# One PSUM copy moved from ScalarE to VectorE, and four row tiles given other memory, in a fused attention and expert kernel

## The chip, the cores and the metric

The kernel runs on one core of one Trainium2 chip. A core has a matrix engine (TensorE, PE in the profile), two engines for elementwise work (VectorE, DVE; ScalarE, ACT), GpSimd (POOL), and a queue engine (SyncE, SP) that here only issues transfers. Each engine works through its own list of instructions in order; semaphores make one wait for another. The metric is the device time of one execution in microseconds.

## The reference

Sliding-window attention with a linear distance bias over 8 batches, 8 heads, 576 positions and 64 channels, and behind it a top-1 mixture of 8 experts over the 4608 tokens, everything in float32:

```python
scores = q @ k.T / sqrt(64) - slope[h] * |i - j|      # only 0 <= i - j < 128
attn   = softmax(scores) @ v                           # (B, H, S, D) -> x (B*S, H*D)
logits = x @ w_gate                                    # 4608 x 8
e      = argmax(logits);  gate_w = softmax(logits)[e]
y      = gate_w * (relu(x @ w1[e]) @ w2[e])            # w1: 512 x 1024, w2: 1024 x 512
```

## The kernel before

**Units.** Attention is cut into 16 units: 4 pairs of batches (`bp`) times 4 pairs of heads (`hp`). A unit has four steps, `g` = 0 to 3. `scores` (L800) multiplies keys and queries into a PSUM tile `sp`; ScalarE takes the exponentials out of it (L811, L816) into `pe`; VectorE multiplies them by distance factors (`weigh`, L830); `values` (L857) multiplies them by V into the PSUM tile `at`. The queries of a unit are taken in two halves of 320 and 256 positions. The first half is complete in step 2, the second in step 3. There is one `at` tile, so the second half's matmuls may not begin before the first half has been copied out. `finish` does that: L874 copies 128 x 640 floats (first half) or 128 x 384 (second half) into `xT`, and L876 the remaining 128 columns of the second half. `sums` (L894) then has TensorE add up the exponentials, and VectorE collects the sums (L907).

**Order.** The order is written by hand: `tc.manual_schedule()` keeps each engine's instructions as the Python code emits them. The main loop emits, per step, the scores of steps ahead, this step's values, and one entry of a list of `tasks`. Steps 0, 1 and 3 take an entry at their end; step 2 takes one just behind `finish` of the first half. So what a step 1 takes stands ahead of that copy on every engine.

**Tasks.** When a pair is done, the tasks of the pair are spread over the following pair's 16 steps (`behind`): gate logits (`gate`, L915 on TensorE and L920, L922 on VectorE), turned by TensorE (`turn`, L939) and copied (L940), then VectorE chains: softmax scales (`scale_a`, L948 onward; `scale_a2`, L969 and L973), the choice of the expert, counting and slots, one-hot tables (`ones_at`, L1063 and L1069; `ones_at2`, L1078), and the rows of `x` written to DRAM. In the first pair the rows are made by VectorE transposes (`squares_turned`, L1158), a small GpSimd copy (L1166) and four transfers of GpSimd's queue for each row tile (`squares_out`, L1177); eight of the nine row tiles take buffers in turn out of a pool of five named `xs`, and the ninth (t = 8) does too. In the later pairs TensorE and ScalarE make the rows (L1107, L1109). `xT` has two buffers, so the third pair's first copy overwrites what the first pair's transposes read.

**The end of attention.** After three pairs the tokens of the first expert are listed (`early_table`, L1100 and L1195 to L1201) and gathered by GpSimd into a tile `s` (L1324). VectorE scales each gathered tile (`to_scale`, L1343), TensorE turns it (L1366), ScalarE copies it (L1367), VectorE forms sums of it (L540 to L543), and the first expert begins (L1619, Strassen's seven products instead of eight). One scaling is a task of the last unit's step 1. The tile `s` has one buffer, which held index numbers at the program's start and nothing from there until this gather.

**The experts.** The rest is seven blocks of matmuls for the experts (L1619, L1684) with their sums on VectorE. `general_path`, the fallback for other routings, is compiled in and not executed.

## Time and profile before

| | |
|---|---|
| median of 3 runs | 637.21 us (635.33 to 641.54) |
| profiled execution | 639.93 us, its span 638.2 us |
| TensorE busy | 603.6 us, 95% of the span |
| VectorE, ScalarE, GpSimd busy | 59%, 33%, 41% |
| granted TensorE clock | 0.993 of full speed |
| attention | 4 to 167 us of the span |

The profile has a page of totals, a list of groups of instructions with the idle time ahead of them, tables of who waited for whom, sums by stretches of time, and a timeline. A timeline row reads: start in us, duration in us (several merged instructions end together), engine, line, operation, tiles written and read, shape and count, and in brackets the time that the engine stood idle before and who ended it. The first matmuls of `values` of unit 4 start at 46.6 us, those of unit 8 at 84.0, of unit 12 at 128.1, of unit 15 at 161.7.

### The profile page before, as it was taken

What the parts mean: (1) busy time and instruction counts of PE and PEld (TensorE: products, weight loads), DVE (VectorE), ACT (ScalarE), POOL (GpSimd) and SP (SyncE); (2) the same over time, 40 slices, a digit from 0 to 9 for tenths busy, and PEclk for the clock granted to TensorE, in tenths of its full rate; (3) what the DMA queues carried; (4) which work ended last, traced back from release to release, by engine and by line L of the source; (5) the groups of instructions that cost most, each with busy time, mean ns of one, the idle gap of its engine ahead of it and who ended that gap; (6) DMA issues with size and microseconds to landing.
All of it is one profiled execution on the core that took longest, in us unless ns stands there. A gap on an engine that the chain in (4) does not pass through costs nothing.

```text
span 638.2 us, 13413 instructions
## 1 busy us (share of the span) xinstructions
PE 603.6 (95%) x5204; PEld 480.9 (75%) x5204; DVE 378.6 (59%) x731; ACT 213.8 (33%) x456; POOL 261.5 (41%) x452
## 2 busy tenths in 40 slices
PE   5889989999889999999999999999999999999995
PEld 4766767777688986777666677777777778999884
DVE  3345966678769682485548455665565575586511
ACT  5767747677332122310330032113202311311310
POOL 8200473405203304873663376258515624840022
PEclk9999999999989999999999999999999999999998
DMA  9895897996605673760466047514822470460212
GB/s 239 232 239 172 239 249 205 368 242 207 200 2 137 189 251 92 288 210 13 91 196 213 17 88 201 212 31 103 299 78 66 132 283 24 103 229 17 46 61 70
DMA packets 80332, 101.09 MB, mean 158 GB/s; under 512 B 41699, under 2 KB 57219, under 8 KB 80259
## 3 DMA queue, kind: packets, MB, share of 16 engines
q1 hardware_dynamic: 68722, 72.08, 38.9%
q0 software_dynamic: 10384, 27.18, 13.8%
q8 instruction: 43, 0.70, 0.5%
q10 hardware_dynamic: 1152, 0.88, 0.5%
q14 instruction: 31, 0.25, 0.1%
HBM read 72.54 MB, written 19.30 MB: 144 GB/s over the span
## 4 chain that ended last, share of the span: by engine, by line
PE 73%; DVE 6%; DMA 5%; issue 5%; ACT 4%; SPq 3%; POOL 2%; POOLq 0%; ACTq 0%; DVEq 0%
PE trio L1684 29%; PE trio L1619 28%; PE sp L800 4%; PE at L857 4%; SPq L1719 3%; PE m L894 3%; DMA q_sb<-in_qT_dram 3%; DMA x_rows<-xs 2%; ACT pe L816 1%; PE m L1107 1%; PE trio L1787 1%; PE trio L1799 1%; ACT pe L811 1%; POOL out_dram L1727 1%; PE m L915 1%
## 5 line engine op out<-in xcount | busy, mean ns | idle before, releaser
L1324 POOL DMA_INDIRECT xg<-x_rows,p_idx x110 | 117.6, 1069 | 29.8 <-issue 26.0
L1610 DVE TENSOR_TENSOR h<-trio,s 128x624 f32<-128x624 f32 (+6 forms) x48 | 35.9, 748 | 92.8 <-PE trio L1619 92.2
L1619 PE MATMUL trio<-xgT,w 128*128 128x312 f32 (+5 forms) x336 | 87.4, 410 | 0.7 <-ACT z L1805 0.7
L1684 PE MATMUL trio<-h,w 128*128 128x312 f32 (+5 forms) x320 | 80.6, 409 | 0.0
L1619 PEld LDWEIGHTS trio<-xgT,w 128*128 128x128 f32 x336 | 63.8, 190 | 20.3 <-ACT z L1805 1.5
L1684 PEld LDWEIGHTS trio<-h,w 128*128 128x128 f32 x320 | 62.5, 196 | 16.0
L830 DVE TENSOR_TENSOR pe<-pe,x 128x512 f32<-128x512 f32 x64 | 43.4, 686 | 33.8 <-ACT pe L811 33.5
L800 PE MATMUL sp<-q_sb,k_sb 64*64 64x192 f32 (+2 forms) x1152 | 55.3, 322 | 8.4 <-DMA q_sb<-in_qT_dram 7.3
L1611 ACT ACTIVATE h<-h 128x624 f32<-128x624 f32 (+6 forms) x48 | 32.6, 678 | 90.9 <-DVE h L1610 90.9
L857 PE MATMUL at<-pe,v_sb 64*64 64x192 f32 (+2 forms) x1408 | 54.4, 284 | 5.5 <-ACT xT L874 3.8
L1619 PE MATMUL trio<-xs,ws 128*128 128x312 f32 (+5 forms) x224 | 57.5, 410 | 0.0
L1684 PE MATMUL trio<-hs,w2s 128*128 128x312 f32 (+5 forms) x224 | 55.8, 407 | 0.0
L857 PEld LDWEIGHTS at<-pe,v_sb 64*64 64x64 f32 x1408 | 45.0, 134 | 13.2 <-ACT xT L874 6.3
L800 PEld LDWEIGHTS sp<-q_sb,k_sb 64*64 64x64 f32 x1152 | 40.0, 137 | 18.4 <-ACT pe L816 4.2
L1619 PEld LDWEIGHTS trio<-xs,ws 128*128 128x128 f32 x224 | 42.6, 190 | 12.6
L1684 PEld LDWEIGHTS trio<-hs,w2s 128*128 128x128 f32 x224 | 43.6, 196 | 10.6
L811 ACT ACTIVATE pe<-sp 128x512 f32<-128x512 f32 x64 | 38.7, 604 | 26.0 <-PE sp L800 21.2
L816 ACT ACTIVATE pe<-sp,mid 128x128 f32<-128x128 f32 x128 | 40.4, 377 | 0.0
L1727 POOL DMA_INDIRECT out_dram<-x,s_idx x19 | 20.5, 1078 | 41.6 <-DMA x<-zo 34.9
L1727 POOL DMA_INDIRECT out_dram<-zo,s_idx x19 | 21.8, 1149 | 25.9 <-DVE zo L1772 15.0
L1619 PE MATMUL trio<-xgT,ws 128*128 128x312 f32 (+5 forms) x112 | 29.9, 410 | 0.0
L1619 PE MATMUL trio<-xs,w 128*128 128x312 f32 (+5 forms) x112 | 29.9, 410 | 0.0
(257 smaller groups left out, 927.0 us busy)
## 6 DMA issues: line engine op xcount, KB each, us to landing
w<-in_moe_w_dram SPq DMA_DIRECT2D x15, 2048.0 KB
k_sb<-in_kT_dram SPq DMA_DIRECT2D x15, 576.0 KB
q_sb<-in_qT_dram SPq DMA_DIRECT2D x15, 576.0 KB
v_sb<-in_v_dram SPq DMA_DIRECT2D x14, 320.0 KB
x_rows<-xs POOLq DMA_DIRECT2D x16, 264.0 KB, 4.8
v_sb<-in_v_dram SPq DMA_DIRECT2D x14, 256.0 KB
zo<-x SPq DMA_DIRECT2D x88, 40.0 KB
w<-in_moe_w_dram SPq DMA_DIRECT2D x5, 512.0 KB
```

The costliest lines, as they stand in the source:

```text
L800: nc.tensor.matmul(by_distance(sp[c * KB : (c + 1) * KB, r, :GC], kb, 0, n), lhsT=k_sb[u][hs, c, kb * KB : (kb + 1) * KB], rhs=q_sb[u][hs, ...
L811: nc.scalar.activation(outer, sp[:, :, :GC].rearrange("p r (j x) -> p r j x", j=3)[:, :, 0:3:2, :], AF.Exp, scale=SCALE,)
L816: nc.scalar.activation(pe[:, r, 1, :], sp[:, r, inner], AF.Exp, bias=mid[:, h0 + r : h0 + r + 1], scale=SCALE,)
L830: nc.vector.tensor_tensor(outer, outer, fac[:, h0 : h0 + 2, : 2 * w].rearrange("p r (j x) -> p r j x", j=2)[:, :, :, : 2 * KB], op=ALU.mult,)
L857: nc.tensor.matmul(acc[r * D : (r + 1) * D, c, lo - q0 : hi - q0].rearrange("p (j x) -> p j x", x=KB), lhsT=v_sb[u // 2][c * KB : (c + 1) ...
L894: nc.tensor.matmul(sm[at_row : at_row + 32, to], lhsT=ind[:, hp, :], rhs=x[:, r, 2, last] if j is None else x[:, r, j, k0 * KB : k1 * KB], ...
L1324: nc.gpsimd.indirect_dma_start(out=to, out_offset=None, in_=where, in_offset=bass.IndirectOffsetOnAxis(ap=idx, axis=0),)
L1610: nc.vector.tensor_tensor(to, ps, u, op=ALU.add)
L1611: nc.scalar.activation(to, to, AF.Relu)
L1619: nc.tensor.matmul(banks[k][:, f, :n2], lhsT=left[m][:, d, fb * P : (fb + 1) * P], rhs=right[m][:, d, :], start=(m in (1, 2, 5) and d == 0 ...
L1684: nc.tensor.matmul(banks[k][:, c, :n2], lhsT=left[m][:, f, c::2], rhs=right[m][:, f, :], start=(m in (1, 2, 5) and f == 0), stop=True, ski ...
L1727: ins = nc.gpsimd.indirect_dma_start(out=out[:, :], out_offset=bass.IndirectOffsetOnAxis(ap=s_idx[:w, g["c0"] + j : g["c0"] + j + 1], axis=0),
```

## The change

The copy of a unit's first half (128 x 640 floats out of PSUM, 16 of them) is done by VectorE instead of ScalarE; the second half's copies stay on ScalarE. Of the first pair's nine row tiles, t = 4 to 7 are turned into one tile of the memory named `s`, which the first expert's gather uses later; t = 0 to 3 and t = 8 keep the pool of five. Number and order of the transfers stay as they are.

```diff
@@ finish
-            nc.scalar.copy(xT[bp][:, hp, : 2 * LQ].rearrange("p (b q) -> p b q", b=2)[:, :, q0 : q0 + n], acc[:, :, :n])
+            copy = nc.vector.tensor_copy if half == 0 else nc.scalar.copy
+            copy(xT[bp][:, hp, : 2 * LQ].rearrange("p (b q) -> p b q", b=2)[:, :, q0 : q0 + n], acc[:, :, :n])
@@ squares
-                if bp in spare and t < TPB - 1:
+                if bp == 0 and 4 <= t < TPB - 1:
+                    if t == 4:
+                        spare[bp] = mx_pool.tile([P, 4, NA, PW], F32, name="s")
+                    xs_of[bp, t] = spare[bp][:, t - 4]
+                elif bp in spare and t < TPB - 1:
```

Where the copy stands in VectorE's list is shown at three places. Lines behind L874 are higher by one in the changed kernel, behind L1149 by five. First VectorE in unit 5 (second unit of the second pair), before, from the multiplication of step 1 on:

```order
L830 TENSOR_TENSOR pe<-pe,x_138 128x2x2x128
L969 RECIPROCAL r<-s 128x72
L973 TENSOR_TENSOR pr<-gsr,r 128x9x32 x2
L982 TENSOR_TENSOR pr<-pr 128x9x32
L983 TENSOR_TENSOR pr<-pr 128x9x16
```

and now:

```order
L830 TENSOR_TENSOR pe<-pe,x_138 128x2x2x128
L970 RECIPROCAL r<-s 128x72
L974 TENSOR_TENSOR pr<-gsr,r 128x9x32 x2
L875 COPY xT<-at 128x2x320
L983 TENSOR_TENSOR pr<-pr 128x9x32
```

The copy stands behind step 1's task (the reciprocal and two products) and ahead of step 2's. Second, VectorE in unit 7 (last unit of the second pair), before, with the tables (`at_col`, `oc`, and `gsr`, the memory of the row table) and the first pair's row transposes:

```order
L1063 TENSOR_TENSOR at_col<-cols_b,rc 128x432
L1069 TENSOR_TENSOR oc<-at_col,tok 128x432 x2
L830 TENSOR_TENSOR pe<-pe,x_138 128x2x2x128
L1078 TENSOR_TENSOR gsr<-cols_b,rc 128x1152
L1158 STREAM_TRANSPOSE xs<-xT 128x4x128 x2
L830 TENSOR_TENSOR pe<-pe,x_138 128x2x2x128 x2
```

and now:

```order
L1064 TENSOR_TENSOR at_col<-cols_b,rc 128x432
L1070 TENSOR_TENSOR oc<-at_col,tok 128x432 x2
L830 TENSOR_TENSOR pe<-pe,x_138 128x2x2x128
L1079 TENSOR_TENSOR gsr<-cols_b,rc 128x1152
L875 COPY xT<-at 128x2x320
L1163 STREAM_TRANSPOSE s<-xT 128x4x128 x2
L830 TENSOR_TENSOR pe<-pe,x_138 128x2x2x128 x2
```

The copy stands behind the 1152-wide row table, and the transposes of t = 4 and 5 write `s`. Third, VectorE in the last unit, before, with the weight sums (`ws`, `w`) and the first scaling of gathered rows (`xn<-s`):

```order
L830 TENSOR_TENSOR pe<-pe,x_138 128x2x2x128 x2
L1343 TENSOR_TENSOR xn<-s 128x512
L534 TENSOR_TENSOR w_1995<-w_1995 128x512
L907 TENSOR_TENSOR sum_of_163<-m,sum_of_163 64x320
L907 TENSOR_TENSOR sum_of_163<-m,sum_of_163 64x256
```

and now:

```order
L830 TENSOR_TENSOR pe<-pe,x_138 128x2x2x128 x2
L1348 TENSOR_TENSOR xn<-s 128x512
L875 COPY xT<-at 128x2x320
L534 TENSOR_TENSOR w_1992<-w_1992 128x512
L908 TENSOR_TENSOR sum_of_163<-m,sum_of_163 64x320
L908 TENSOR_TENSOR sum_of_163<-m,sum_of_163 64x256
```

The copy stands behind the scaling, which needs the gather's landing. On TensorE, GpSimd and SyncE the order is the same in both kernels; ScalarE's list is the old one without the 16 copies.

## The prediction

> **What bounds the kernel now.** The page's totals come first, then its chain of waits by engine.

> ```profile
> PE 603.6 (95%) x5204; PEld 480.9 (75%) x5204; DVE 378.6 (59%) x731; ACT 213.8 (33%) x456; POOL 261.5 (41%) x452
> PE 73%; DVE 6%; DMA 5%; issue 5%; ACT 4%; SPq 3%; POOL 2%; POOLq 0%; ACTq 0%; DVEq 0%
> ```

> TensorE sets the time, so a change is worth what it takes from TensorE's idle time, or adds to it. Both edits lie in attention, the first 169 us. The table of waits for TensorE from 20 to 175 us says what its idle time there waits for (us in total, times, longest).

> ```profile
> PE at L857 <- ACT xT L874: 3.8, 8, 0.9
> PE m L939 <- DVE gs L920: 2.2, 2, 2.0
> PE m L1366 <- DVE xn L1343: 1.9, 1, 1.9
> ```

> The first line is the copy that changes engine: at 8 of 16 units the second half's matmuls wait for it, 3.8 us in all. The sums by stretches (PE, PEld, DVE, ACT, POOL busy) show how full the two engines are.

> ```profile
> 20.00:40.00 20.00, 17.67 (x467) 14.90 (x460) 9.92 (x18) 15.45 (x45) 0.01 (x1) 1.00 0.92 222
> 60.00:80.00 20.00, 18.13 (x454) 14.99 (x450) 18.23 (x49) 14.55 (x41) 7.62 (x16) 1.00 0.84 238
> ```

> Ahead of the first pair's tasks VectorE is half free (9.92 of 20 us). From 60 to 80 us it is the fuller engine, 18.23 of 20 us, and three units copy there.

> **What the copy costs.** Groups by shape (count, busy us, mean ns):

> ```profile
> L874 ACT COPY xT<-at 128x640 f32<-128x640 f32 x16 | 11.3, 704 | 2.7 <-DVE xs L1158 1.8 <-PE at L857 0.8
> L920 DVE TENSOR_TENSOR gs<-m,sum_of 128x512 f32<-128x512 f32 x8 | 5.5, 689 | 3.6 <-PE m L915 3.6
> L922 DVE TENSOR_TENSOR gs<-m,sum_of 128x128 f32<-128x128 f32 x4 | 1.1, 283 | 0.0
> L907 DVE TENSOR_TENSOR sum_of<-m,sum_of 64x320 f32<-64x320 f32 x12 | 5.8, 482 | 12.6 <-PE m L894 12.6
> L671 DVE CAST pe<-s 128x320 f32<-128x320 int32 x1 | 0.3, 334 | 2.4 <-POOL s L663 2.4
> ```

> ScalarE loses 16 x 0.70 = 11.3 us. VectorE has no 640-wide copy out of PSUM, so its price is bounded: from L922 to L920, both out of PSUM, 384 elements cost 406 ns, 1.06 ns each, and 128 more than L920's give 689 + 135 = 824 ns. Two of the 320-wide casts would be 0.67 us, two of L907's 0.96. I take 0.82 (L920 is nearest), so VectorE gains 13.1 us. [...]

> **Where the copy is no longer late.** With a free VectorE it starts when the first half is done. In unit 2:

> ```profile
> 31.71 0.22 PE L857 MATMUL at<-pe,v_sb 64*64 64x64 f32 x1
> 32.34 0.69 DVE L830 TENSOR_TENSOR pe<-pe,x 128x512 f32<-128x512 f32 x1 [1.03 <-ACT pe L811]
> 32.68 0.73 ACT L874 COPY xT<-at 128x640 f32<-128x640 f32 x1
> 33.46 1.55 PE L857 MATMUL at<-pe,v_sb 64*64 64x64 f32 x48 [0.88 <-ACT xT L874]
> ```

> The half is done at 31.93; ScalarE, busy with exponentials, copies from 32.68. VectorE is free then and its multiplication at 32.34 now stands behind the copy (it is for the next unit, some 4 us later, which hides the delay). Copy 31.99 to 32.81, the matmuls at 32.86 instead of 33.46: gain 0.60. Units 1 and 3 have the same form:

> ```profile
> 24.00 1.55 PE L857 MATMUL at<-pe,v_sb 64*64 64x64 f32 x48 [0.44 <-ACT xT L874]
> 39.19 0.84 PE L857 MATMUL at<-pe,v_sb 64*64 64x192 f32 x24
> 41.23 0.56 PE L857 MATMUL at<-pe,v_sb 64*64 64x64 f32 x15 [0.56 <-ACT xT L874]
> ```

> Unit 1 gains its whole 0.44; unit 3, whose half is done at 39.19 + 0.84 = 40.03 and would be copied by 40.91, gains 0.27. Together 1.3. Units 0, 4, 8 and 13 show no idle time of TensorE for the copy and keep none.

> **Where it now stands behind a task.** VectorE works in order, and step 1's task is ahead of the copy. Unit 5:

> ```profile
> 61.63 0.83 DVE L973 TENSOR_TENSOR pr<-gsr,r 128x288 f32<-128x288 f32 x2
> 61.86 1.55 PE L857 MATMUL at<-pe,v_sb 64*64 64x64 f32 x48 [0.56 <-ACT xT L874]
> ```

> The products end at 62.46; the copy, overlapping their end by 0.07 as VectorE's rows do, ends at 63.2, and the matmuls start at 63.25 instead of 61.86: loss 1.4. Unit 7:

> ```profile
> 79.79 1.35 DVE L1078 TENSOR_TENSOR gsr<-cols_b,rc 128x1152 bf16<-128x1152 bf16 x1
> 78.80 0.89 PE L857 MATMUL at<-pe,v_sb 64*64 64x64 f32 x24 [0.15 <-ACT xT L874]
> 79.92 0.89 PE L857 MATMUL at<-pe,v_sb 64*64 64x192 f32 x24 [0.24 <-DVE pe L830]
> ```

> The row table ends at 81.14, the copy at 81.9, so 78.80 becomes 81.94: 3.1 lost, 2.9 with the 0.24 wait at 79.92 that is then long over. Behind it queue the multiplications for unit 8 and L907, which VectorE catches up while TensorE stands.

> **The row tiles.** Here the second edit enters:

> ```profile
> 87.14 1.07 PE L915 MATMUL m<-xT,wgd 128*32 128x512 f32 x8
> 88.94 0.71 DVE L1158 STREAM_TRANSPOSE xs<-xT 128x512 f32<-128x512 f32 x1 [1.67 <-DMA x_rows<-xs]
> 90.14 0.68 DVE L920 TENSOR_TENSOR gs<-m,sum_of 128x512 f32<-128x512 f32 x1
> 90.88 0.66 PE L939 MATMUL m<-ident,gs 128*128 128x128 f32 x4 [2.04 <-DVE gs L920]
> ```

> The transpose of t = 8 waits 1.67 us for the transfer that empties t = 3's buffer; L920 is queued behind it and TensorE's L939 behind that, idle 2.04. Now t = 8 is only the fifth tile of its pool and waits for nothing. GpSimd still issues the same transfers in the same order, and the tile `s` is idle until its gather, at 161 us. So the second edit alone could return 2.0. Next late is the gate itself: delayed by 2.9, L915 ends at 88.21 + 2.9 = 91.1, L920 at 91.85, and L939 starts at 91.9 instead of 90.88. Of unit 7's 2.9 us, 1.0 remains.

> **The remaining units.** Unit 11 has a row table ahead again:

> ```profile
> 119.58 1.35 DVE L1078 TENSOR_TENSOR gsr<-cols_b,rc 128x1152 bf16<-128x1152 bf16 x1
> 121.33 1.25 PE L857 MATMUL at<-pe,v_sb 64*64 64x64 f32 x33
> ```

> It ends at 120.93, the copy at 121.68: 0.4 lost. For units 6, 9, 10 and 12, where task or copy ends within 0.2 us of TensorE's next matmuls, I estimate 0.3 together. Units 14 and 15:

> ```profile
> 157.45 1.55 PE L857 MATMUL at<-pe,v_sb 64*64 64x64 f32 x48 [0.16 <-ACT xT L874]
> 157.79 0.17 DVE L1201 CAST s_idx<-tb 128x4 int32<-128x4 f32 x1
> 161.16 1.06 POOL L1324 DMA_INDIRECT s<-x_rows,g_idx  x1 [3.86 <-DVE sum_of L907]
> 164.06 1.55 PE L857 MATMUL at<-pe,v_sb 64*64 64x64 f32 x48 [0.85 <-ACT xT L874]
> 165.59 0.69 DVE L1343 TENSOR_TENSOR xn<-s 128x512 f32<-128x512 f32 x1 [1.95 <-DMA s<-x_rows,g_idx]
> ```

> In unit 14 the eight small instructions of the first expert's list end at 157.96; the copy ends at 158.72 and TensorE is 1.3 late. In unit 15 the scaling L1343 waits for the gather until 165.59. It ends at 166.28, the copy at 167.03, and the last matmuls of attention start at 167.08 instead of 164.06. The gather hangs on the rows and the list, both ahead of unit 14's copy, so it does not shift with the 1.3: both units together lose 3.0. The tail keeps it:

> ```profile
> 167.11 0.94 DVE L907 TENSOR_TENSOR sum_of<-m,sum_of 64x320 f32<-64x320 f32 x2 [0.23 <-PE m L894]
> 168.69 1.29 DVE L1343 TENSOR_TENSOR xn<-s 128x512 f32<-128x512 f32 x2
> 169.53 0.63 PE L1366 MATMUL m<-ident,xn 128*128 128x128 f32 x4 [1.89 <-DVE xn L1343]
> ```

> The next scaling stands behind L907, which waits for the last sums on TensorE, 3.0 later too. The experts behind are bound by TensorE and carry it to the end.

> **Sum.** -1.3 + 1.4 + 1.0 + 0.4 + 0.3 + 3.0 = +4.8 us, 0.75%. The profiled execution took 639.93 us with a span of 638.2; it would be 644.7. It lies 2.7 above the median of the runs, which becomes 637.21 + 4.8 = 642.0.

> **Rivals.** First, faster: VectorE reaches the copies in time, so all 3.8 us of waits go, and 2.0 at the row tiles: -5.8, 631.4 us. It decides where step 1's task ends before the first half does; units 1 to 3 speak for it, the rows at 79.79 and 165.59 against. Chance 0.12. Second, no change to speak of: the 3.0 us at the end are taken back, because the first expert's start has waits of its own (1.89 at 169.53 is one): +1.8, 639.0. The order through L907 speaks against. Chance 0.18. Third, slower than forecast: unit 7's 2.9 is kept whole, because VectorE, full from 60 to 80 us, enters unit 8 as late as TensorE does (+1.9), and the copy costs 0.96 (0.14 at 7 places, +1.0): +7.7, 644.9. L907's waits of 12.6 us in all speak against, since VectorE catches up there. Chance 0.15. Nothing suggests that the edits do not do what they say; the order shows both.

> **Numbers.** The forecast has 0.55. One per cent is 6.4 us, about what a measurement tells from no change. Two of the copies at 0.67 instead of 0.82 and the runs' own spread (635.33 to 641.54) put it between 638.5 and 645.5. The range 636.0 to 646.0 holds forecast, second and third rival and leaves out the first and some of the third's tail. Slower by over 1% (643.6) takes a quarter of the forecast and most of the third rival, 0.26; faster by over 1% half of the first, 0.06; within 1% the rest, 0.68.

> **What would show it.** The 640-wide copy as a VectorE group near 0.82 us; TensorE's waits at L857 for VectorE's copy near 1.4 (unit 5), 3 (unit 7), 1.4 and 2.5 us (units 14, 15) and none in units 1 to 3; no wait of the t = 8 transpose for a transfer; attention ending 4 to 5 us later. It is wrong if these copies end within 0.2 us of where ScalarE's did, or if the first expert's sums (L540) start as early as before.

## The result and the profile after

The changed kernel took 647.65 us, the median of 5 runs (645.78 to 649.93), against 637.21 us before, which is now also the median of 5: a ratio of 1.0145, 95% interval 1.0115 to 1.0174. (Ratios here leave out disturbed runs, so they need not be the quotients of the medians.) The forecast was 642.0 us with a range from 636.0 to 646.0. The direction was right, the result lies above the range, and the loss was about twice the 0.75% forecast. The profiled execution took 647.65 us, its span is 645.9, against 639.93 and 638.2: 7.7 us more where +4.8 was forecast.

The page's totals and its chain by engine, the table of waits from 20 to 175 us, and the copy's group:

```profile
PE 607.9 (94%) x5204; PEld 482.9 (75%) x5204; DVE 389.9 (60%) x747; ACT 204.4 (32%) x440; POOL 259.7 (40%) x452
PE 76%; DVE 8%; issue 5%; SPq 3%; DMA 2%; ACT 2%; POOL 1%; POOLq 0%; ACTq 0%; DVEq 0%
...
PE at L857 <- DVE xT L875: 10.1, 8, 3.4
...
L875 DVE COPY xT<-at 128x640 f32<-128x640 f32 x16 | 13.1, 822 | 5.6 <-PE at L857 5.4
```

The copy costs what was forecast, 0.822 us. TensorE's wait for it grew from 3.8 to 10.1 us in as many places (8), the longest from 0.9 to 3.4. TensorE's busy time grew too, by 4.3 us, although it executes the same 5204 matmuls; 2.6 us of that lie in unit 7, as shown below. Matmuls that take longer are what the prediction did not have.

Where a task stands ahead of the copy, the timeline shows the row that the order foretold. Unit 2 (VectorE free), unit 5, and units 14 and 15:

```profile
31.62 0.82 DVE L875 COPY xT<-at 128x640 f32<-128x640 f32 x1 [0.64 <-PE at L857]
32.50 1.55 PE L857 MATMUL at<-pe,v_sb 64*64 64x64 f32 x48 [0.30 <-DVE xT L875]
...
60.98 0.83 DVE L974 TENSOR_TENSOR pr<-gsr,r 128x288 f32<-128x288 f32 x2
61.72 0.82 DVE L875 COPY xT<-at 128x640 f32<-128x640 f32 x1
62.59 1.22 PE L857 MATMUL at<-pe,v_sb 64*64 64x64 f32 x32 [1.94 <-DVE xT L875]
...
163.39 0.82 DVE L875 COPY xT<-at 128x640 f32<-128x640 f32 x1
164.26 1.55 PE L857 MATMUL at<-pe,v_sb 64*64 64x64 f32 x48 [1.44 <-DVE xT L875]
...
170.62 0.69 DVE L1348 TENSOR_TENSOR xn<-s 128x512 f32<-128x512 f32 x1 [0.17 <-DMA s<-x_rows,g_idx]
171.34 0.82 DVE L875 COPY xT<-at 128x640 f32<-128x640 f32 x1
172.22 1.55 PE L857 MATMUL at<-pe,v_sb 64*64 64x64 f32 x48 [2.19 <-DVE xT L875]
```

Unit 7 and the gate behind it:

```profile
80.81 1.34 DVE L1079 TENSOR_TENSOR gsr<-cols_b,rc 128x1152 bf16<-128x1152 bf16 x1
82.19 0.82 DVE L875 COPY xT<-at 128x640 f32<-128x640 f32 x1
83.07 2.84 PE L857 MATMUL at<-pe,v_sb 64*64 64x64 f32 x48 [3.44 <-DVE xT L875]
85.84 2.79 PE L895 MATMUL m<-pe,ind 128*32 128x320 f32 x28
92.91 0.70 DVE L1163 STREAM_TRANSPOSE xs<-xT 128x512 f32<-128x512 f32 x1
95.40 0.66 PE L940 MATMUL m<-ident,gs 128*128 128x128 f32 x4 [0.18 <-DVE gs L921]
96.68 1.50 PE L857 MATMUL at<-pe,v_sb 64*64 64x64 f32 x48
```

The wait of 3.44 us is the one forecast, and so is the end of the gate's wait: the transpose of t = 8 waits for nothing, and L940 for 0.18 us instead of 2.04. (Whether the row tiles did that is seen below, where the copies move alone.) But the two groups of matmuls behind the wait took 2.84 and 2.79 us. The same 48 matmuls of unit 14 took 1.55, and the 28 of the sums 1.51 there. The sums by stretches show why; the granted clock is the third number from the end of each row. Before, then after:

```profile
80.00:100.00 20.00, 17.63 (x366) 13.02 (x370) 12.64 (x27) 11.08 (x30) 16.09 (x33) 1.00 0.91 241
```

```profile
80.00:100.00 20.00, 16.75 (x305) 12.18 (x305) 13.21 (x22) 7.34 (x21) 15.66 (x34) 0.83 0.86 232
81.70:88.60 6.90, 5.53 (x77) 4.29 (x78) 3.67 (x6) 0.65 (x2) 4.46 (x11) 0.51 0.89 250
```

TensorE's clock was halved for 6.8 us, from inside the wait until 88.5 us. (2.84 - 1.55) + (2.79 - 1.51) = 2.6 us were lost on work that waits for nothing. That is more than the gate gave back: from unit 7's second half to unit 8's it took 96.68 - 83.07 = 13.61 us. Before it took 92.17 - 78.80 = 13.37:

```profile
92.17 1.50 PE L857 MATMUL at<-pe,v_sb 64*64 64x64 f32 x48
```

The lag of the changed kernel, that is, how much later than before the second halves' matmuls start in the two timelines: -1.21 us at unit 3, -0.65 at unit 4, +0.73 at unit 5, +4.27 at unit 7, +4.51 at unit 8, +5.37 at unit 11, +5.38 at unit 13, +6.81 and +8.16 at units 14 and 15, +7.8 at the first expert's sums and +7.75 at the end.

### The profile page after: what moved, and what is told of

Same layout as the page of the kernel before. It is cut to its first block, busy times and chain, and to the rows that moved or that the text cites. A ratio compares the mean times of both kernels' runs of the same rounds, so it can differ in the third digit from the quotient of the medians.

```text
span 645.9 us, 13410 instructions
## 1 busy us (share of the span) xinstructions
PE 607.9 (94%) x5204; PEld 482.9 (75%) x5204; DVE 389.9 (60%) x747; ACT 204.4 (32%) x440; POOL 259.7 (40%) x452
## 3 DMA queue, kind: packets, MB, share of 16 engines
q10 hardware_dynamic: 1152, 0.88, 0.5%
## 4 chain that ended last, share of the span: by engine, by line
PE 76%; DVE 8%; issue 5%; SPq 3%; DMA 2%; ACT 2%; POOL 1%; POOLq 0%; ACTq 0%; DVEq 0%
PE trio L1689 29%; PE trio L1624 27%; PE at L857 6%; PE sp L800 5%; PE m L895 3%; SPq L1724 3%; PE m L1108 1%; DVE xT L875 1%; PE trio L1792 1%; PE trio L1804 1%; PE m L916 1%; DMA q_sb<-in_qT_dram 1%; POOL out_dram L1732 1%; DVE pe L830 1%; DVE xT L1163 1%
## 5 line engine op out<-in xcount | busy, mean ns | idle before, releaser
L1624 PE MATMUL trio<-xgT,w 128*128 128x312 f32 (+5 forms) x336 | 87.4, 410 | 0.7 <-ACT z L1810 0.7
L1624 PEld LDWEIGHTS trio<-xgT,w 128*128 128x128 f32 x336 | 63.8, 190 | 20.3 <-ACT z L1810 1.5
L857 PE MATMUL at<-pe,v_sb 64*64 64x192 f32 (+2 forms) x1408 | 56.3, 290 | 11.9 <-DVE xT L875 10.1
L857 PEld LDWEIGHTS at<-pe,v_sb 64*64 64x64 f32 x1408 | 45.9, 138 | 21.1 <-DVE xT L875 14.3
L830 DVE TENSOR_TENSOR pe<-pe,x 128x512 f32<-128x512 f32 x64 | 43.3, 686 | 24.2 <-ACT pe L811 23.9
L1624 PE MATMUL trio<-xs,ws 128*128 128x312 f32 (+5 forms) x224 | 57.5, 410 | 0.0
L1624 PEld LDWEIGHTS trio<-xs,ws 128*128 128x128 f32 x224 | 42.6, 190 | 12.6
L811 ACT ACTIVATE pe<-sp 128x512 f32<-128x512 f32 x64 | 38.5, 601 | 31.9 <-PE sp L800 26.9
L1624 PE MATMUL trio<-xs,w 128*128 128x312 f32 (+5 forms) x112 | 29.9, 410 | 0.0
L1624 PE MATMUL trio<-xgT,ws 128*128 128x312 f32 (+5 forms) x112 | 29.9, 410 | 0.0
```

The source lines that it names most:

```text
L811: nc.scalar.activation(outer, sp[:, :, :GC].rearrange("p r (j x) -> p r j x", j=3)[:, :, 0:3:2, :], AF.Exp, scale=SCALE,)
L830: nc.vector.tensor_tensor(outer, outer, fac[:, h0 : h0 + 2, : 2 * w].rearrange("p r (j x) -> p r j x", j=2)[:, :, :, : 2 * KB], op=ALU.mult,)
L857: nc.tensor.matmul(acc[r * D : (r + 1) * D, c, lo - q0 : hi - q0].rearrange("p (j x) -> p j x", x=KB), lhsT=v_sb[u // 2][c * KB : (c + 1) ...
L1624: nc.tensor.matmul(banks[k][:, f, :n2], lhsT=left[m][:, d, fb * P : (fb + 1) * P], rhs=right[m][:, d, :], start=(m in (1, 2, 5) and d == 0 ...
```

## The experiments

The theory that the two profiles suggest: VectorE's order makes the waits as forecast, and the wait of 3.4 us in unit 7 has a second price, the halved clock behind it, which takes what the row tiles give. Rivals: the row edit returns nothing; the wait alone is the loss, whatever the clock does; the loss lies mostly elsewhere (units 14 and 15). Four groups of four kernels, each group beside the kernel before on its own chip (the first group has no run of the changed kernel):

| kernel | median, us | before, us | ratio (95% interval) |
|---|---|---|---|
| row tiles alone | 649.74 | 649.46 | 0.9989 (0.9950 to 1.0029) |
| copies alone | 655.73 | 649.46 | 1.0105 (1.0065 to 1.0146) |
| changed, unit 7's copy on ScalarE | 651.23 | 649.46 | 1.0040 (1.0023 to 1.0057) |
| changed, unit 7's wait filled | 650.03 | 649.46 | 1.0031 (1.0004 to 1.0057) |
| changed | 653.61 | 648.64 | 1.0071 (1.0030 to 1.0113) |
| changed, units 14 and 15 on ScalarE | 655.92 | 648.64 | 1.0116 (1.0063 to 1.0170) |
| VectorE only where it is free | 648.69 | 648.64 | 0.9976 (0.9934 to 1.0019) |
| changed, step 1's task behind the copy | 647.02 | 648.64 | 0.9993 (0.9960 to 1.0026) |
| changed | 654.27 | 648.35 | 1.0123 (1.0082 to 1.0163) |
| changed, unit 7's wait filled | 651.88 | 648.35 | 1.0058 (1.0023 to 1.0094) |
| VectorE in unit 7 alone | 651.86 | 648.35 | 1.0051 (1.0017 to 1.0085) |
| VectorE where free, and two waits filled | 645.92 | 648.35 | 0.9995 (0.9957 to 1.0034) |
| changed | 654.26 | 648.86 | 1.0071 (1.0036 to 1.0105) |
| changed, units 14 and 15 on ScalarE | 653.40 | 648.86 | 1.0045 (1.0006 to 1.0083) |
| VectorE in units 14 and 15 alone | 646.42 | 648.86 | 0.9940 (0.9907 to 0.9973) |
| row tiles alone | 646.24 | 648.86 | 0.9941 (0.9901 to 0.9981) |

### The two edits apart

Row tiles alone, run twice:

```diff
-            copy = nc.vector.tensor_copy if half == 0 else nc.scalar.copy
+            copy = nc.scalar.copy
```

> Only the row tiles t = 4 to 7 take the other memory; all copies stay on ScalarE. My theory (the row edit removes the 1.67 us wait of the t = 8 transpose and TensorE's 2.04 us wait behind it): 2.0 us less than before, about 635.2 against 637.2, and no idle time of TensorE over 0.5 us ahead of the gate's first transposes. Rival (the wait is hidden anyway): within 0.5 us of before.

> All copies on ScalarE; only the four row tiles as in the changed kernel. In the trace 1.7 us less than before at the gate, from unit 7's second half to unit 8's 11.6 us instead of 13.4; a ratio to the kernel before of 0.997 if that is kept to the end, 1.000 if it is not.

The timeline of the second run, from unit 7's second half to unit 8's:

```profile
77.98 0.89 PE L857 MATMUL at<-pe,v_sb 64*64 64x64 f32 x24 [0.15 <-ACT xT L875]
...
86.41 0.70 DVE L1163 STREAM_TRANSPOSE xs<-xT 128x512 f32<-128x512 f32 x1
...
88.34 0.66 PE L940 MATMUL m<-ident,gs 128*128 128x128 f32 x4 [0.28 <-DVE gs L921]
...
89.63 1.50 PE L857 MATMUL at<-pe,v_sb 64*64 64x64 f32 x48
```

11.65 us (11.64 in the first run) instead of 13.37: the row edit returns 1.7 us of the 2.0 forecast for it alone. The times show no clear difference in the first run (0.9989, where 2.0 us or 0.3% less was expected) and 0.6% in the second (0.9941, where 0.997 or 1.000 was), so its size at the end is known only as between nothing and some 4 us (0.6% of 648).

Copies alone, with the row tiles as before:

```diff
-                if bp == 0 and 4 <= t < TPB - 1:
-                    if t == 4:
-                        spare[bp] = mx_pool.tile([P, 4, NA, PW], F32, name="s")
-                    xs_of[bp, t] = spare[bp][:, t - 4]
-                elif bp in spare and t < TPB - 1:
+                if bp in spare and t < TPB - 1:
```

> Only the copies move to VectorE; all row tiles use the pool of five. My theory: as the changed kernel or up to 2 us slower, 647 to 650, since the stalls all come from the copies and the row wait is then added to them or hidden behind them. Rival (the row tiles in the other memory cause part of the loss): 2 us or more faster than the changed kernel, 645.5 or less.

1.0105, with a wait of 3.46 us in unit 7 and 3.41 us of half clock, most of it behind that wait. So the copies make the loss by themselves; the row edit is not needed for it. The expectation is in times of the first comparison's chip, and the times of this chip can't decide it. The gate's wait is gone in this kernel too, although its row tiles are those of before:

```profile
90.87 0.70 DVE L1159 STREAM_TRANSPOSE xs<-xT 128x512 f32<-128x512 f32 x1
...
93.36 0.66 PE L940 MATMUL m<-ident,gs 128*128 128x128 f32 x4 [0.18 <-DVE gs L921]
```

The delay at unit 7 has already let the transfer land that t = 8 waited for. From unit 7's second half to unit 8's this kernel takes 12.39 us, and the changed kernel 12.48 in the profile of the third group, which has as much half clock. So the row edit returns 1.7 us where the copies stay on ScalarE, and nothing that these traces show where unit 7's copy is late.

### Unit 7: the wait, and the clock behind it

First, unit 7's copy back on ScalarE; second, the wait kept but filled with five matmuls of 128 x 320 into a PSUM tile that nothing reads (`KB` is 64; run twice); third, VectorE in unit 7 alone.

```diff
+            copy = nc.vector.tensor_copy if half == 0 and u != 7 else nc.scalar.copy
```
```diff
+                if u == 7:
+                    idle = ps_m.tile([P, 512], F32, name="m")
+                    for _ in range(5):
+                        nc.tensor.matmul(idle[:, : 5 * KB], lhsT=ident[:], rhs=fac[:, 0, : 5 * KB], start=True, stop=True)
                 values(u, 1, (3, 4, 5))
```
```diff
+            copy = nc.vector.tensor_copy if half == 0 and u == 7 else nc.scalar.copy
```

> The changed kernel with the copy of unit 7 alone left on ScalarE. Theory (TensorE's 3.44 us stall there also halves its clock for the next 6.8 us, so that the matmuls behind it take 2.8 us instead of 1.5, twice): the stall's 3.2 us and the clock's 2.6 us go, 5 to 6 us less than the changed kernel, about 642, and no stretch of half clock between 60 and 170 us. Rival (the prediction's: the stall is mostly given back at the gate, net 1.0 us): about 1 us less, 646.5.

> The changed kernel with five extra matmuls (identity times 320 columns of the distance factors, into a PSUM tile that nobody reads; they add work and nothing to the output) in TensorE's list just ahead of the second half's matmuls of unit 7. They occupy about 3 us of the 3.4 us in which TensorE waits for the copy, and nothing else moves. Theory (the idle time halves the clock): the clock stays full there, the matmuls behind take 1.5 us again, and the kernel is about 2.6 us faster than the changed one, 645. Rival (clock not the cause, matmuls there are slow because of something else): no gain, or slower by what sticks out of the filler.

> The changed kernel once more, timed beside the three kernels that follow. Theory: TensorE idle about 3.4 us ahead of unit 7's second half, and a stretch of half clock of 3.41 or 6.83 us that begins inside that idle time; ratio to the kernel before between 1.007 and 1.015 (the two earlier comparisons). Rival (the first comparison's loss was mostly a matter of its chip): under 1.005.

> The changed kernel with five added matmuls of 128x320 on TensorE ahead of unit 7's second half, into a PSUM tile that nothing reads; they fill the idle time and change no output. Clock theory: no half clock between 78 and 92 us, unit 7's second half to unit 8's 11.0 us instead of 12.6 to 13.6, and the median 1.3 to 2.6 us below the changed kernel's of the same chip. Rival (the idle time alone is the loss, whatever the clock does): unit 7's second half starts no earlier, so no difference to the changed kernel, within 0.5 us.

> VectorE copies the first half in unit 7 alone, ScalarE in the other fifteen; the four row tiles as in the changed kernel. Clock theory: +3.2 us of idle time ahead of unit 7's second half, a stretch of half clock behind it, and 0.6 to 1.5 us of these given back at the gate: from unit 6's second half to unit 8's 23 to 25 us (before 21.2), +2 to +3.5 us at the end of attention, a ratio of 1.003 to 1.006. Rival (the prediction's term): 1.9 given back, +1.0 us, from unit 6's second half to unit 8's 22.2, a ratio of 1.0015.

With unit 7's copy on ScalarE, unit 6's second half to unit 8's took 19.37 us, in the changed kernel 24.64: 5.3 less (5 to 6 expected), and no half clock between 60 and 165 us. In time its 1.0040 lies clear of the 1.0105 of the copies alone on the same chip, though these differ in the row tiles as well. The rows of the first filled run (the first is that of the five added matmuls, which the profile counts as ten):

```profile
80.14 2.96 PE L1502 MATMUL m<-x,ident 128*128 128x320 f32 x10
83.66 1.55 PE L857 MATMUL at<-pe,v_sb 64*64 64x64 f32 x48 [0.55 <-DVE xT L875]
85.13 1.51 PE L895 MATMUL m<-pe,ind 128*32 128x320 f32 x28
...
94.70 1.50 PE L857 MATMUL at<-pe,v_sb 64*64 64x64 f32 x48
```

This separates wait and clock: the second half's matmuls still wait for the copy, but take 1.55 and 1.51 us, and unit 8's follow 11.04 us later instead of 13.61. The second filled run has the same 11.04, and the changed kernel on its chip 12.48, with 3.41 us of half clock. From unit 6's second half to unit 8's both filled runs take 22.07 us, 0.9 more than the 21.16 of before: with the clock whole, the 1.0 us that the prediction put on unit 7 comes out. In time, the second chip's medians are 651.88 and 654.27, 2.4 us less than the changed kernel (expected 1.3 to 2.6; the intervals of the two ratios just overlap), and on the first filled run's chip its 1.0031 lies clear of the 1.0105 of the copies alone. So added work made this stretch of the trace shorter, and by all signs the kernel too. The rival by which the wait alone is the loss falls.

VectorE in unit 7 alone:

```profile
80.24 1.62 PE L857 MATMUL at<-pe,v_sb 64*64 64x64 f32 x48 [3.45 <-DVE xT L875]
81.79 2.79 PE L895 MATMUL m<-pe,ind 128*32 128x320 f32 x28
...
92.85 1.50 PE L857 MATMUL at<-pe,v_sb 64*64 64x64 f32 x48
```

From unit 6 to unit 8 it took 23.70 us (expected 23 to 25, by the prediction's term 22.2; before 21.16), and the ratio is 1.0051 (expected 1.003 to 1.006). So unit 7 costs 2.5 us in the trace, and by the ratio 3.3 (its interval goes from 1.1 to 5.5), where the prediction put 1.0, row edit included. Here the clock fell behind the wait, at 81.58 us, when the matmuls had already begun again at 80.24. That led to a count over all profiles, in the last section.

### Which copies VectorE can take

VectorE in units 1, 2, 3, 8, 12 and 13 only, and the whole change with step 1's task emitted behind the copy:

```diff
+            copy = nc.vector.tensor_copy if half == 0 and u in (1, 2, 3, 8, 12, 13) else nc.scalar.copy
```
```diff
                 finish(u, 0)
+                some()
                 some()
...
-            if g != 2:
+            if g not in (1, 2):
                 some()
```

> The changed kernel once more, as the measure for the others here, since chips differ. All theories: 1.2 to 1.7% above before. In the trace, theory (clock): where TensorE's idle time in unit 7 covers one or two of the trace's clock stretches of 3.4 us, the matmuls behind take 2.8 us instead of 1.5; unit 7 to unit 8 then takes 12.4 us (one stretch) or 13.6 us (two).

> The changed kernel with VectorE copying only in units 1, 2, 3, 8, 12 and 13, where no long task stands ahead of the copy; the other ten copies on ScalarE; row tiles as changed. Theory (the loss is only the copies queued behind tasks): the changed kernel's whole loss goes and the small gains stay, 0.5 us in units 2 and 3 and 1.7 at the gate: 1 to 2.5 us faster than before, ratio 0.996 to 0.999. Rival (VectorE's added work itself is the loss): slower than before.

> The changed kernel, all 16 copies on VectorE, but the task of a unit's step 1 emitted behind the first half's copy, with the task of step 2, on all engines. Theory (place in the list, not VectorE's load, is the loss): no idle time of TensorE over 0.5 us ahead of the second halves of units 5, 7 and 14, and none over 1 us in unit 15; 2 to 5 us faster than before, ratio 0.992 to 0.997. Rival (VectorE is too full from 60 to 80 us): idle time returns as waits for the distance multiplications there, and the kernel is no faster than before.

Against the changed kernel's 1.0071 on that chip (1.2 to 1.7% was expected of it) they have 0.9976 and 0.9993: the loss is gone in both, and in the second by the place of the copy alone, since all 16 copies stay on VectorE. Neither is measurably faster than before, which was expected of both; of all the kernels only the row tiles alone, and with units 14 and 15, came out faster, on one chip. With the task behind, unit 5's wait is back at 0.56 us and unit 14's is gone. Unit 7's is 2.13, where 0.5 at most was expected, since VectorE is behind there even without the row table. Unit 15's is 2.24, but there VectorE itself stood idle for 1.13 us ahead of the copy. The rows of unit 7:

```profile
77.10 0.68 DVE L830 TENSOR_TENSOR pe<-pe,x 128x512 f32<-128x512 f32 x1
77.81 0.82 DVE L875 COPY xT<-at 128x640 f32<-128x640 f32 x1
78.56 1.35 DVE L1079 TENSOR_TENSOR gsr<-cols_b,rc 128x1152 bf16<-128x1152 bf16 x1
78.69 1.49 PE L857 MATMUL at<-pe,v_sb 64*64 64x64 f32 x44 [2.13 <-DVE xT L875]
```

A last kernel took the first of these and filled two waits of the first expert's start, with two and three added matmuls whose results are written over before they are read:

```diff
+                if g.get("early") and j == 1:
+                    for _ in range(2):
+                        nc.tensor.matmul(tp[:, :320], lhsT=ident[:], rhs=g["w1"][:, 0, :320], start=True, stop=True)
...
+                    if g.get("early") and p == 0 and m == 6:
+                        for _ in range(3):
+                            nc.tensor.matmul(banks[2][:, 0, :320], lhsT=ident[:], rhs=w[:, 0, :320], start=True, stop=True)
```

> VectorE copies only in units 1, 2, 3, 8, 12 and 13, where nothing of a task stands ahead of it; the four row tiles as in the changed kernel; and two and three added matmuls of 128x320 into PSUM that is written again before it is read, at two waits of the first expert's start. They change no output. Theory: the gain of the six copies and the row tiles (2 to 3 us) plus 1.7 us for each stretch of half clock that the filled waits no longer bring about between 168 and 190 us: a ratio of 0.992 to 0.996, and no half clock from 168 to 190 us. Rival (the waits were no cause of the clock there, or the added matmuls delay the first expert by as much as they save): a ratio of 0.997 to 1.000.

Half clock is gone from 169.1 to 636.8 us (a stretch that began at 165.7 us, ahead of the filled waits, reaches into the window of the expectation), and L1624's wait of 2.09 us in the kernel without the filling became

```profile
181.39 1.78 PE L1630 MATMUL trio<-x,ws 128*128 128x224 f32 x8 [0.47 <-DVE x L541]
```

but the ratio, 0.9995, is the rival's: no gain that can be measured, though the median is 2.4 us below that of the kernel before.

### Units 14 and 15

Undone alone (twice), and done alone:

```diff
+            copy = nc.vector.tensor_copy if half == 0 and u not in (14, 15) else nc.scalar.copy
```
```diff
+            copy = nc.vector.tensor_copy if half == 0 and u in (14, 15) else nc.scalar.copy
```

> The changed kernel with the copies of units 14 and 15 left on ScalarE. Theory (in these two the copy waits for the list and for the gathered rows): TensorE's 1.4 and 2.2 us ahead of their second halves fall to the 0.2 and 0.9 of before, 2.8 us less than the changed kernel (0.45%). Rival (the first expert's start takes such a delay back): no difference over 0.5 us.

> The changed kernel, timed beside the three kernels that follow. A ratio to the kernel before of 1.007 to 1.015; TensorE waits 1.4 us in unit 14 and 1.8 to 2.2 us in unit 15 for VectorE's copy.

> The changed kernel with the copies of units 14 and 15 back on ScalarE. Theory (the prediction's 3.0 us for these units is kept to the end): median 2.5 to 3.5 us below the changed kernel's of the same chip, a ratio of about 1.007 where the changed kernel has 1.012. Rival (the first expert's start has waits of its own that take the 3.0 back, or the copies are no cause): within 1 us of the changed kernel.

> VectorE copies the first half in units 14 and 15 alone, ScalarE in the other fourteen; the four row tiles as in the changed kernel. Theory: waits of 1.4 us in unit 14 and 1.8 to 2.2 us in unit 15, and a median 2.5 to 3.5 us above the next kernel's. Rival: within 1 us of the next kernel's.

Undoing them was expected to save some 3 us. It gave 1.0045 against 1.0071 on one chip, 1.7 us less with intervals that overlap. On the other the ratio rose to 1.0116; that trace has a wait of 3.57 us for ScalarE's copy in unit 15, ahead of which ScalarE itself stood idle for 2.79 us, and half clock from inside that wait on (the first 16 matmuls behind it took 0.92 us, where unit 14's 48 take 1.55 at full clock). Doing them alone was expected to cost as much and shows no cost: 0.9940 against 0.9941 for the row tiles alone, but the intervals reach 2 to 3 us to either side, so a cost of 3 us is not excluded. The timelines of this last pair, VectorE's kernel first:

```profile
163.55 0.90 PE L857 MATMUL at<-pe,v_sb 64*64 64x192 f32 x22 [0.39 <-issue]
164.91 0.68 DVE L1348 TENSOR_TENSOR xn<-s 128x512 f32<-128x512 f32 x1
165.63 0.82 DVE L875 COPY xT<-at 128x640 f32<-128x640 f32 x1
166.51 2.84 PE L857 MATMUL at<-pe,v_sb 64*64 64x64 f32 x48 [2.05 <-DVE xT L875]
174.55 0.63 PE L1371 MATMUL m<-ident,xn 128*128 128x128 f32 x4 [1.77 <-DVE xn L1348]
```

```profile
161.32 0.56 PE L857 MATMUL at<-pe,v_sb 64*64 64x192 f32 x5 [0.19 <-issue]
165.07 0.49 PE L857 MATMUL at<-pe,v_sb 64*64 64x64 f32 x3 [0.47 <-issue]
166.34 2.84 PE L857 MATMUL at<-pe,v_sb 64*64 64x64 f32 x48 [0.78 <-ACT xT L875]
173.85 0.87 PE L1371 MATMUL m<-ident,xn 128*128 128x128 f32 x4 [1.90 <-DVE xn L1348]
```

In these executions TensorE comes to the first half's last products late by itself, through waits that nothing in the profile releases ("issue"). Without VectorE's copy they go on until 165.07, so the second half starts at 166.34 anyway. In the first comparison's two profiles neither kernel has such waits in unit 15 (40 matmuls in 1.49 us), and the trace shows 2.8 of the 3.0 us. Between the two traces VectorE's kernel is still 2.4 us behind from unit 13 to the end of attention (30.2 and 27.8 us), 1.9 of them by the start of unit 15's second half and the rest by where half clock falls (the 28 matmuls of the sums took 2.79 and 2.26 us), and 1.0 at the first expert's sums, after a stretch of half clock that only the kernel without the copies has (the gate's 24 matmuls took 2.31 and 3.53 us). So the wait is shown, and that it reaches the end of the kernel on every chip is not: its size there stays open, between 0 and 3 us.

## Why the prediction was right, and where it failed

**What bounds it, and the mechanism.** Right: TensorE is the bound (busy 95% of the span before, 94% after), and a late copy is worth what it leaves TensorE idle. The copy's price, 0.82 us, was measured at 0.822, so the third rival's 0.96 was wrong.

**Units 1 to 3 (-1.3).** -1.21 at unit 3, so right, though waits of 0.17 to 0.30 us remain where the text's last part said none; 0.56 of the gain was gone again at unit 4, which the sum did not have: within unit 3's second half a wait of TensorE that the profile ends by "issue" grew from 0.79 to 1.25 us.

**Unit 5 (+1.4), unit 11 (+0.4), the small ones (+0.3).** +1.38, +0.57, and +0.6 for units 6, 9, 10, 12 and 13.

**Units 14 and 15 (+3.0).** +2.78 in the first comparison's traces, and the tail kept it there as the order through L907 said. That the gather does not shift with unit 14's wait was right: the scaling starts at 170.62, 5.03 us later than before, which is less than the lag at unit 13. The later chips confirm the waits but not that their price always arrives.

**Unit 7 and the row tiles: the step that failed.** "Of unit 7's 2.9 us, 1.0 remains." The wait itself was right (+3.24 against 3.1), and so were the 0.24 and 1.9 us that come back behind it (2.3 in the filled kernels), though the 1.9 was credited to the row tiles and the late copy brings it back without them. The step put at nothing, and without a reason, what a wait of 3.4 us does to the clock: 2.6 us were lost behind it in this profile, 1.4 in the changed kernel's third profile, which has 3.41 us of half clock there. So +3.5 remained instead of +1.0, and that is 2.5 of the 2.9 us between the profiled +7.7 and the sum's +4.8. The filled kernels show it apart from everything else: with the clock whole +0.9 remains.

**The rivals.** The first two fell. The third is nearest in number (644.9), by luck: it had VectorE enter unit 8 late and the gate wait on, and L940 waited 0.18 us. No rival spoke of the clock, though the profile before showed a wait of TensorE of 2.45 us, up to 179.38 us, and half clock for 3.41 us from 179.07 on.

**What is left over.** The measured ratio is 1.0145 in the first comparison, and 1.0071, 1.0123 and 1.0071 in the later ones, with the forecast at 1.0075. The mean of the four is 1.0103, some 6.6 us of the kernel before. The forecast's size was thus low by about 2 us on average, about what unit 7's clock took, and by about 4 in the first comparison. There 1.5 us between the profiled pair (7.7) and the ratio (9.2) are not explained by the profiles. With unit 7's clock in the sum it would have been 4.8 + 2.5 = 7.3 us, or 644.5, inside the range; that the median went beyond 646.0 is in part left open.

## What to carry to other kernels

Before an operation moves to an engine with time to spare, look at what stands ahead of it in that engine's list at each place, not at the engine's share of busy time: the same copy gains 0.5 us in unit 2 and loses 3.2 in unit 7. A wait of TensorE of 3.4 us counted twice in all 8 profiles that have it in unit 7: the wait, and the matmuls behind it at half clock for 3.41 or 6.83 us, 2.6 us of loss in the first comparison's profile and 1.4 in the third group's. Around 2 us it went either way: a wait of 2.09 us in the changed kernel (up to 187.17 us) was followed by 3.41 us of half clock, one of 2.13 with step 1's task behind the copy by none. Where such a wait can't be removed, matmuls that nobody needs, put into it, can cost less than leaving it empty, as they did in unit 7 (11.04 us to unit 8's second half instead of 12.48 on the same chip); at the first expert's start they kept the clock whole and brought no gain that can be measured.

## What the runs showed of the hardware

**Half clock came in stretches of 3.41 or 6.83 us.** All stretches of half clock inside the work of the 18 profiled executions last that long, and within one execution they begin whole multiples of 3.413 us apart, with waits and matmuls alike between them. In the changed kernel's first profile they run from 81.72 to 88.55 us and from 187.53 to 190.95, and the two starts lie 31.00 times 3.413 us apart. A window here is one such step of 3.413 us, counted from where an execution's half clock starts. In VectorE-in-unit-7-alone, two neighbouring windows:

```profile
78.17:81.58 3.41, 1.34 (x48) 1.30 (x48) 3.38 (x5) 0.00 (x0) 2.04 (x6) 1.00 1.05 287
81.58:84.99 3.41, 3.41 (x47) 2.46 (x40) 1.33 (x3) 0.65 (x2) 3.12 (x7) 0.50 0.89 286
```

TensorE was idle for 2.07 us of the first window, and the next one ran at half clock although TensorE worked all through it. In the kernel with step 1's task behind the copy, the wait of 2.13 us lies across a border of two windows:

```profile
74.16:77.57 3.41, 2.25 (x56) 1.61 (x52) 3.38 (x7) 2.83 (x9) 2.66 (x7) 1.00 0.86 226
77.57:80.99 3.42, 2.30 (x64) 2.03 (x68) 3.39 (x5) 0.81 (x3) 2.87 (x7) 1.00 1.06 287
80.99:84.40 3.41, 3.41 (x89) 2.81 (x83) 3.35 (x8) 1.35 (x4) 1.64 (x3) 1.00 1.03 299
```

**The kernel before differs between comparisons by more than the change.** Its median was 637.21 us in the first comparison and 648.4 to 649.5 in the four groups that followed, each on a chip of its own. All 16 profiles of these groups have "issue" waits of TensorE between 155 and 178 us, 0.7 to 1.8 us in all, and the two of the first comparison have none. That is a small part of the 11 us; the rest, and whether the chip is the cause, is not shown.
